# A step's sum over head groups and its turn as one fp32 product with a selector, in a recurrent attention kernel

## The chip, the cores and the metric

One core of a Trainium2 chip runs the whole program. The metric is the device time of one execution in microseconds (us); the time of a kernel is the median of several executions. Engines are named as in the profile: PE is TensorE's matrix multiplication and PEld its weight load, DVE is VectorE, ACT is ScalarE, POOL is GpSimd, SP is the engine that issues most DMAs.

## The reference, cut to what matters

The reference is one forward and backward pass of a layer that adds three things: the input, a squared-ReLU feed-forward block on the normalised input, and an attention that runs over 64 segments of 32 rows, each with 8 rows of memory that the segment before it has made. The gradients of all inputs are returned as well, so the recurrence is run once forward and once backward.

```python
for s in range(n_seg):                       # 64 segments, one after the other
    xs = x[:, s * seg_len:(s + 1) * seg_len, :].copy()
    h = jnp.concatenate([mem, xs], axis=1)   # 8 + 32 rows of 512
    q = jnp.einsum('btd,dhe->bhte', h, Wq)   # 32 heads of 128
    k = jnp.einsum('btd,dhe->bhte', h, Wk)
    v = jnp.einsum('btd,dhe->bhte', h, Wv)
    scores = jnp.einsum('bhqe,bhke->bhqk', q, k) * scale
    scores = jnp.where(mask[None, None], scores, -1000000000.0)
    p = _softmax(scores, axis=-1)
    o = jnp.einsum('bhqk,bhke->bhqe', p, v)
    o = jnp.einsum('bhte,hed->btd', o, Wo)   # a sum over the 32 heads
    mem = o[:, :M, :].copy()                 # the next segment starts from this
    outs.append(o[:, M:, :])
```

The last product is a sum over all 32 heads. Its first 8 rows are what the next segment waits for. In the backward pass the gradient of the memory goes the other way, segment 63 first, and the sum over heads (of the products with Wq, Wk and Wv turned) closes each step in the same way.

## The kernel before, in words

The program has five stages: the feed-forward block; its weight gradients; the forward recurrence; a short pass over left-over rows; the backward recurrence; and last the attention's weight gradients. On the timeline of the profile the forward recurrence lies at about 423 to 1342 us and the backward one at about 1578 to 2545 us.

A recurrence has 64 steps, in 16 blocks of 4 (`SPB` is 4, `NB` 16). In a step the 32 heads lie as 4 groups of 8 (`HG` is 4): partitions 32g to 32g + 31 hold the 32 rows of group g. A step projects its rows (`proj`, line 421, 4 column tiles at a time), turns them (`flip`, line 165), makes scores (`scores`, line 442), softmax or its gradient on DVE and ACT (`soft_ops`, `ds_ops`), the products with the values (`outer`, line 549) and the product with the output weights (`gather`, line 462). `gather` leaves in the PSUM tile `ps_R` (forward) or `ps_gR` (backward) 128 rows of 512: for each group g its own partial sum over 8 heads, 32 rows each.

The end of a step makes of this the turned sum over the groups. Its operations, by their names in the order lists:

- `ra`, `rb`: the two halves of the 128 x 512 partial sums are copied from PSUM to the fp32 tile `R4` ("R" in the profile), one by DVE (line 408), one by ACT (line 405), one after the other. Which half comes first differs from step to step.
- `ta`, `tb` (`turn_ops`, line 471): four fp32 transposes by TensorE, two for each half, into one PSUM tile `ps_sum` of 128 x 512. Column c * 128 + 32g + r of it belongs to chunk c of the model dimension, group g, row r.
- `HT` (`over_groups`, line 484): one DVE sum over g of rows 0 to 7 into the next step's input (`X` forward, `GT` backward). The next step's projections wait for it.
- `xt` (`over_groups` again): the same for rows 8 to 31 into the block's fp32 tile `XT` (`b_XT` backward).

The 8 memory rows of four steps are also handled once per block together ("left" rows, order names with `L.`): `L.ta` and `L.tb` make the same four transposes from `R4L` or `b_R`, and `L.xt` (`left_sums`, line 478) sums them with four DVE instructions.

The order of all this is written out by hand: `F_ORDER` and `B_ORDER` list the names of the operations for the four steps of a block, `play` calls them in that order, and each engine gets its instructions in it. A `+` or `-` behind a name moves it to another step; `L.` names belong to the block. What is put behind `ta` and `tb` in these lists (a gather of left rows of 8 or 16 matmuls, `L.G0` or `L.H1` and the like, a score `L.S1+`, products `L.W1+`) runs on TensorE while DVE does `HT`. `on_engines` says which copies are done by ACT and which by DVE. PSUM tiles named by `big` and `tr` share four banks that are given out in turn.

```python
"L.ta kl k1fl soN-- k0Te q1Te L.tb s0 ..."          # forward, fourth step, left products among the flips
"... qg1 rb L.G3 L.ldt+ tb ra ta L.H3 HT"           # backward, third step's end
"ldk- ldp- vp0 L.ko0 vp1 s0 L.tb- L.ldk L.xt- d10"  # backward, a block's first step: L.xt stands before d10 on DVE
```

`d10` to `d40` are the four DVE instructions of the scores' gradient (lines 498 to 508).

Of the kernel before, what the change touches and what calls it, by code (L numbers as in the profile page):

```python
# [8 lines left out]
ALU = mybir.AluOpType  # L9
AX = mybir.AxisListType  # L10
BF16 = mybir.dt.bfloat16
F32 = mybir.dt.float32
P = 128
# [13 lines left out]
def kernel(  # L27
# [27 lines left out]
    nc = tc.nc  # L55

    _, S, D = A_x.shape
    M = A_mem0.shape[1]
    H, Dh = A_Wq.shape[1], A_Wq.shape[2]
    F = B_w1.shape[1]  # L60
    SEG = int(A_seg_len)
    assert Dh == P and D % P == 0 and F % P == 0 and S % P == 0 and D <= 512
    L = M + SEG
    assert L <= 64 and P % SEG == 0
    NSEG = S // SEG
    DC = D // P
    TC = S // P
    HD = H * Dh
    SPB = P // SEG
# [29 lines left out]
    const = ctx.enter_context(tc.tile_pool(name="const", bufs=1))  # L99
# [3 lines left out]
    HG = 4  # L103
# [48 lines left out]
    nc.vector.memset(ones_col[:], 1.0)  # L152
    identF = const.tile([P, P], F32, name="identF")
    nc.vector.tensor_copy(identF[:], ident[:])
    rstd_t = const.tile([P, TC], F32, name="rstd_t")

    def sb(name, bufs, side=None):
# [12 lines left out]
    HT = htp.tile([P, DC, S], BF16, name="HT")  # L170
# [8 lines left out]
    with sb("p1", 1) as p1, sb("p1b", 2) as p1b:  # L179
# [64 lines left out]
        for rb in range(NRB):  # L244
# [4 lines left out]
            for fc in range(FC):  # L249
                ps = pst([P, RB], F32, name="ps_h1")  # L250
                for dc in range(DC):
                    nc.tensor.matmul(ps[:], lhsT=W1[:, dc, fc * P:(fc + 1) * P], rhs=HT[:, dc, r0:r0 + RB],
                                     start=(dc == 0), stop=(dc == DC - 1))
                nc.scalar.activation(rT[:, fc, :], ps[:], ACT.Relu, bias=b1T[:, fc:fc + 1], scale=1.0)
                nc.vector.tensor_tensor(out=aT[:, fc, :], in0=rT[:, fc, :], in1=rT[:, fc, :], op=ALU.mult)
            for fc in range(FC):
                ps2 = pst([P, RB], F32, name="ps_ga")
                for dc in range(DC):
                    nc.tensor.matmul(ps2[:], lhsT=W2T[:, dc, fc * P:(fc + 1) * P], rhs=gT[:, dc, r0:r0 + RB],
                                     start=(dc == 0), stop=(dc == DC - 1))  # L260
# [23 lines left out]
            for rc in range(RCB):  # L284
                rr0 = r0 + rc * P
                psB = pst([P, D], F32, name="ps_B")
                for fc in range(FC):
                    nc.tensor.matmul(psB[:], lhsT=aT[:, fc, rc * P:(rc + 1) * P], rhs=W2[:, fc, :],
                                     start=(fc == 0), stop=(fc == FC - 1))
# [6 lines left out]
                for fc in range(FC):  # L296
                    nc.tensor.matmul(psG[:], lhsT=gh1T[:, fc, rc * P:(rc + 1) * P], rhs=W1T[:, fc, :],
                                     start=(fc == 0), stop=(fc == FC - 1))
# [3 lines left out]
                for srcT, dstD in ((aT, S_AN), (gh1T, S_GH1N)):  # L302
                    Nt = p1b.tile([P, F], BF16, name="Nt", tag="Nt")
                    for (f0b, nb) in GRPF8:
                        ps = pst([P, nb * P], BF16, name="ps_trf")
# [13 lines left out]
    with sb("p2", 1) as p2:  # L319
# [5 lines left out]
        with sb("p2r", 1, "right") as p2r:  # L325
# [19 lines left out]
            ps = pst([1, D], F32, name="ps_gb2")  # L345
# [120 lines left out]
    def turn_ops(o, alloc, R4, st):  # L466

        def tT(c):
            if "T" not in st:
                st["T"] = alloc("ps_sum")  # L470
            nc.tensor.transpose(st["T"][:, c * P:(c + 1) * P], R4()[:, c * P:(c + 1) * P], identF[:])  # L471
        for h in range(2):
            o["t%s" % "ab"[h]] = lambda h=h: [tT(c) for c in (2 * h, 2 * h + 1)]

    def left_sums(XT, T):

        for c in range(DC):
            nc.vector.tensor_reduce(XT[:, c, :, 0:M], T[:, c * P:(c + 1) * P].rearrange("p (g j t) -> p j t g", g=HG, j=SPB),
                                    axis=AX.X, op=ALU.add)

    def over_groups(out, T, rows):

        with nc.allow_low_precision(reason="summed in float32, rounded once on the way out"):
            nc.vector.tensor_reduce(out, T[:].rearrange("p (c g r) -> p c r g", c=DC, g=HG)[:, :, rows], axis=AX.X,  # L484
                                    op=ALU.add)

    def block_rows(ps, XT):

# [94 lines left out]
    def play(order, n, steps, lefts, step, blk, last={}):  # L583
# [34 lines left out]
        "ob1+ L.tu1+ g1+ ra+ soP+ ws+ L.u0 soN L.W0+ L.BT rb+ L.E0+ L.E1+ ta+ tb+ L.ob0+ soN+ L.W1+")  # L618
    ENGS = on_engines(
        "L.E0 L.E1 L.E3 L.E4 L.E5 L.oa1 L.ob1 k0ev k1ev oa0 ob0 ob1 q0ev q1Te q1ev rb v0ev v1ev",  # L620
        "L.E2 L.oa0 L.ob0 L.pm0 L.pm1 L.ra k0Te k1Te oa1 pm0 pm1 q0Te ra we")
    with sb("fw", 1) as fw, psum("fr", 4) as fr, psum("fpp", 1) as fpp, \
            ExitStack() as fstack:

# [45 lines left out]
        def block(b):  # L670

            if b not in blk:
                shapes = {"kL": (fs, [P, KH, HG, NL], BF16), "OT": (fs, [P, HG, KH, SPB, SEG], BF16),
                          "X": (fs, [P, DC, P], BF16),
                          "kM": (fo, [P, KH, HG, NL], BF16), "vTM": (fo, [P, KH, HG, NL], BF16),
                          "XT": (fs, [P, DC, SPB, SEG], F32), "qL": (fo, [P, KH, HG, NL], BF16),
                          "VL": (fo, [P, GW], BF16), "vM": (fo, [P, GW], BF16), "EL": (fo, [P, KH, KW], BF16),
                          "OTL": (fo, [P, KH, HG, NL], BF16),
                          "bb": (fo, [P, D], BF16)}

                def make(n):
                    pool, shape, dt = shapes[n]
                    return pool.tile(shape, dt, name=n, tag=n)
                blk[b] = Tiles(make)
            return blk[b]
# [114 lines left out]
        def fwd(s):  # L800
# [88 lines left out]
            def HTf():  # L889
                if s + 1 < NSEG:  # L890
                    b1, j1 = divmod(s + 1, SPB)
                    over_groups(block(b1)["X"][:, :, j1 * SEG:j1 * SEG + M], st["T"], slice(0, M))
            o["HT"] = HTf
            o["xt"] = lambda: over_groups(B_["XT"][:, :, j, M:SEG], st["T"], slice(M, SEG))
            t, h0 = divmod(2 * s, H)

            def wt():
# [58 lines left out]
    with sb("ls", 3) as ls, sb("lo", 1) as lo_, psum("lpp", 1) as lpp, psum("lr", 4) as lr:  # L956
# [99 lines left out]
        "o1mm+ o0fl+ L.qo0+ L.ta o0te+ o1ev+ L.ko1+")  # L1056
    ENGS = on_engines(
        "L.ra0 kea0 kea1 keb0 kla0 klb0 o0ev o1ev o1te qea0 qea1 rb vea veb vla vlb",
        "keb1 kla1 klb1 o0te qeb0 qeb1 ra")
    with sb("bq", 1) as bq, sb("bs", 2) as bs, sb("bt", 1) as bt, psum("bpp", 1) as bpp, psum("br", 4) as br:  # L1060
        G4 = {n: bq.tile([P, HG, KH, SPB, SEG], BF16, name="g" + n) for n in "vkq"}
        gS = bq.tile([P, KH, KW], BF16, name="gS")
# [96 lines left out]
        def bwd(s):  # L1159
# [106 lines left out]
            def HTf():  # L1266
                if s > 0:
                    b1, j1 = divmod(s - 1, SPB)
                    over_groups(gts[b1][:, :, j1 * SEG:j1 * SEG + M], st["T"], slice(0, M))
                else:  # L1270
                    ps["S0"] = bq.tile([P, DC, M], F32, name="gm0")
                    over_groups(ps["S0"][:], st["T"], slice(0, M))
            o["HT"] = HTf

            def xtf():
                over_groups(B_["XT"][:, :, j, M:SEG], st["T"], slice(M, SEG))
            o["xt"] = xtf
            o["S0"] = lambda: ps["S0"]
            return o
# [170 lines left out]
```

## Time and profile before

| What | Value |
|---|---|
| median of 7 runs | 3193.85 us (3180.56 to 3206.58) |
| the profiled execution | 3186.18 us, span 3184.4 us |
| mean granted TensorE clock | 0.943 of full speed |
| PE busy, matmuls | 2726.6 us (86%), 51480 |
| PEld busy, weight loads | 1393.5 us (44%), 51480 |
| DVE busy, instructions | 1250.4 us (39%), 3503 |
| ACT busy, instructions | 1019.3 us (32%), 2370 |
| DMA engines | 594.37 MB, 187 GB/s in the mean |

The table is of one profiled execution. A busy share is a share of the span; TensorE's matmuls are pipelined, so that its busy time says that it had work, not that it ran at its peak. In a line of the groups, such as "L471 PE MATMUL ps_sum<-identF,R 128*128 128x128 f32 x512 | 100.3, 295 | 22.6 <-ACT R L405 16.1", stand the line of the program, the engine, the operation, what it writes and reads, its shape, the number of instructions, their busy time in us, the mean length of one in ns, and the engine's idle time just before them with what ended most of it. In the view of a tile the three numbers are the shortest, median and longest length in ns. On the timeline the first number is the start in us, the second the length from the first to the last end of the instructions that the line stands for.

### The profile page before, as it was taken

The numbers are of one execution on the slowest core, as the hardware profiler recorded it, in microseconds if no ns is written. First come the engines' busy times: TensorE is split into PE (matmuls) and PEld (weight loads), VectorE is DVE, ScalarE is ACT, GpSimd is POOL, SyncE is SP. The second block draws the span as 40 slices with busy tenths as digits, with TensorE's granted clock in tenths as the row PEclk, the third lists the DMA queues.
The fourth block names the chain that finished last, engine by engine and source line by source line (L and its number), as shares of the span: only waits on it lengthen the run. The fifth ranks groups of instructions, "written<-read, shape, count | busy, mean of one in ns | idle before, by whom it ended". The sixth has DMA issues, their size and how long they took to land.

```text
span 3184.4 us, 115139 instructions
## 1 busy us (share of the span) xinstructions
PE 2726.6 (86%) x51480; PEld 1393.5 (44%) x51480; DVE 1250.4 (39%) x3503; ACT 1019.3 (32%) x2370; POOL 329.7 (10%) x601
## 2 busy tenths in 40 slices
PE   8998789999999988635688888898899847999998
PEld 4553345545555544312344444444444423444443
DVE  5540055556666656423344444444445400010011
ACT  2331144444445444212333333333333201111111
POOL 0000010000000000000122222222122100000000
PEclk9999899999999999766799999999999978999999
DMA  9358636667677766689666777677677599999993
GB/s 255 124 131 311 241 110 183 194 179 196 175 195 195 194 181 155 205 209 251 164 156 185 174 168 187 173 166 185 169 174 184 160 251 196 215 190 220 188 185 90
DMA packets 827697, 594.37 MB, mean 187 GB/s; under 512 B 595633, under 2 KB 705346, under 8 KB 824002
## 3 DMA queue, kind: packets, MB, share of 16 engines
q1 hardware_dynamic: 809794, 532.47, 67.5%
q0 software_dynamic: 17408, 54.54, 5.8%
q8 instruction: 403, 6.60, 0.9%
q14 instruction: 92, 0.75, 0.1%
HBM read 205.14 MB, written 250.10 MB: 143 GB/s over the span
## 4 chain that ended last, share of the span: by engine, by line
PE 63%; DMA 11%; SPq 8%; DVE 8%; ACT 5%; issue 4%; POOL 0%; ACTq 0%; POOLq 0%; DVEq 0%
PE ps_gw L1411 13%; PE ps_proj L421 12%; PE ps_gR L462 9%; PE b_pp L549 4%; PE ps_sum L471 3%; SPq L1336 3%; DMA S_GOL<-l_gON 3%; PE ps_R L462 3%; PE ps_L L382 2%; PE ps_tr L165 2%; PE ps_RL L1115 2%; PE ps_w L341 2%; PE ps_w L361 2%; PE ps_sc L442 1%; PE f_pp L549 1%
## 5 line engine op out<-in xcount | busy, mean ns | idle before, releaser
L1411 PE MATMUL ps_gw<-gn,HNc 128*128 128x512 bf16 x1920 | 416.7, 379 | 3.4 <-ACT wt L1386 3.4
L421 PE MATMUL ps_proj<-Wqkv,X 128*32 128x512 bf16 x6144 | 367.2, 389 | 16.6 <-DVE X L484 6.9
L1411 PEld LDWEIGHTS <-HNc 128*128 128x128 bf16 x1920 | 187.8, 98 | 227.6 <-issue 4.0
L405 ACT CAST f_N<-ps_proj 128x512 bf16<-128x512 f32 x384 | 218.6, 587 | 188.6 <-PE ps_proj L421 178.8
L1386 ACT CAST wt<-ps_gw 128x512 bf16<-128x512 f32 x126 | 69.6, 591 | 547.4 <-DMA out_dram<-wt 310.1
L421 PEld LDWEIGHTS <-X 128*32 128x32 bf16 x6144 | 161.2, 98 | 172.5 <-issue 20.3
L1369 DVE TENSOR_TENSOR gx<-ps_rows,gb 128x512 f32<-128x512 f32 x16 | 11.1, 692 | 434.4 <-PE ps_rows L1367 434.4
L1411 PE MATMUL ps_gw<-GOc,gn 128*128 128x512 bf16 x640 | 141.9, 385 | 28.1 <-DMA gn<-S_ON 28.1
L462 PE MATMUL ps_gR<-WT,gv 128*32 128x512 bf16 x2048 | 149.2, 386 | 9.2 <-ACT gOT L405 4.2
L462 PE MATMUL ps_gR<-WT,gk 128*32 128x512 bf16 x2048 | 142.4, 397 | 11.4 <-ACT gk L405 6.0
L462 PE MATMUL ps_gR<-WT,gq 128*32 128x512 bf16 x2048 | 143.7, 402 | 5.6 <-issue 5.4
L421 PE MATMUL ps_proj<-WoT,GT 128*32 128x512 bf16 x2048 | 124.0, 384 | 5.1 <-POOL GT L1145 4.0
L405 ACT CAST gON<-ps_proj 128x512 bf16<-128x512 f32 x128 | 75.0, 586 | 166.2 <-PE ps_proj L421 166.2
L462 PE MATMUL ps_R<-Wo,OT 128*32 128x512 bf16 x2048 | 123.1, 382 | 0.0
L471 PE MATMUL ps_sum<-identF,R 128*128 128x128 f32 x512 | 100.3, 295 | 22.6 <-ACT R L405 16.1
L829 POOL COPY kM<-f_kT 128x256 bf16<-128x256 bf16 x64 | 25.8, 403 | 831.0 <-DVE f_kT L408 831.0
L382 PE MATMUL ps_L<-Wqkv,XL 128*128 128x512 bf16 x384 | 96.9, 388 | 16.6 <-DMA XL<-S_XL 16.6
L1411 PEld LDWEIGHTS <-gn 128*128 128x128 bf16 x640 | 63.4, 99 | 105.5 <-DMA gn<-S_ON 28.4
L405 ACT CAST gk<-b_pp 128x256 bf16<-128x256 f32 x192 | 65.9, 381 | 134.3 <-PE b_pp L549 126.2
L471 PEld LDWEIGHTS ps_sum<-identF,R 128*128 128x128 f32 x512 | 55.3, 142 | 84.8 <-ACT R L405 59.3
L408 DVE COPY R<-ps_gR 128x256 f32<-128x256 f32 x64 | 27.2, 425 | 162.3 <-ACT R L405 118.4
L405 ACT CAST OT<-f_pp 128x256 bf16<-128x256 f32 x192 | 65.2, 374 | 63.4 <-PE f_pp L549 62.4
(221 smaller groups left out, 4659.8 us busy)
## 6 DMA issues: line engine op xcount, KB each, us to landing
S_A<-f_N SPq DMA_DIRECT2D x64, 512.0 KB
out_dram<-wt SPq DMA_DIRECT2D x154, 128.0 KB
S_A<-f_N SPq DMA_DIRECT2D x64, 256.0 KB
S_ON<-OC SPq DMA_DIRECT2D x64, 256.0 KB
b_qN<-S_A POOLq DMA_DIRECT2D x64, 256.0 KB, 4.3
b_kN<-S_A POOLq DMA_DIRECT2D x64, 256.0 KB, 4.0
S_GB<-gv SPq DMA_DIRECT2D x32, 512.0 KB
S_GB<-gq SPq DMA_DIRECT2D x32, 512.0 KB
```

Source lines behind the costliest of these rows:

```text
L165: nc.tensor.transpose(ps_ap, in_ap, ident[base:base + k, base:base + k])
L341: nc.tensor.matmul(ps[:], lhsT=aN[:, rc, fc * P:(fc + 1) * P], rhs=gN[:, rc, :], start=(rc == 0), stop=(rc == TC - 1))
L361: nc.tensor.matmul(ps[:, 0:nf], lhsT=xnN[:, rc, dc * P:(dc + 1) * P], rhs=gh1N[:, rc, f0:f0 + nf], start=(rc == 0), stop=(rc == TC - 1))
L382: nc.tensor.matmul(ps[:], lhsT=x(dc), rhs=Wqkv[:, dc, c0:c0 + 512], start=(dc == 0), stop=(dc == DC - 1))
L405: nc.scalar.copy(out, in_)
L421: nc.tensor.matmul(ps[32 * g:32 * g + 32, :], lhsT=hT[:, dc, :], rhs=W[:, dc, c:c + 4 * P], start=(dc == 0), stop=(dc == DC - 1), tile_pos ...
L462: nc.tensor.matmul(R[32 * g:32 * g + 32, :], lhsT=XT(k, g), rhs=W[:, g * KH + k, :], start=(first and k == 4 * h), stop=(last and k == 4 * ...
L471: nc.tensor.transpose(st["T"][:, c * P:(c + 1) * P], R4()[:, c * P:(c + 1) * P], identF[:])
L549: nc.tensor.matmul(o, lhsT=N_[32 * g:32 * g + m, kk * P:(kk + 1) * P], rhs=X(kk)[32 * g:32 * g + m], start=(i == 0), stop=(i == len(jobs) ...
L1336: nc.sync.dma_start_transpose(t_[:, b, :].rearrange("p (k e) -> p k e", k=KH), blocks(b)[:, g].rearrange("p k r -> p (k r)"))
L1386: nc.any.tensor_copy(wt[:], ps[:])
L1411: nc.tensor.matmul(ps[:], lhsT=l(rc), rhs=r(rc), start=(n == 0), stop=(n == RC_ALL - 1))
```

## The change

`sel` is a 128 x 32 fp32 tile: four 32 x 32 identities under each other, made at the start by one DVE sum over the four column groups of the identity. In place of a transpose, each chunk of `R4` becomes the stationary operand of a true fp32 matmul with `sel` as the moving one: this turns the chunk and sums the four groups at once, and leaves 32 columns in place of 128. `HT`, `xt` and `L.xt` then only copy from PSUM; they stay on DVE (`HT xt L.xt` are added to the DVE names of both stages), and `L.xt` is one copy in place of four sums. The order lists are not changed. Line numbers of the changed program are higher by 2 above this place and lower by 2 below it.

```diff
--- before.py
+++ after.py
@@ -152,6 +152,8 @@
     nc.vector.memset(ones_col[:], 1.0)
     identF = const.tile([P, P], F32, name="identF")
     nc.vector.tensor_copy(identF[:], ident[:])
+    sel = const.tile([P, SEG], F32, name="sel")
+    nc.vector.tensor_reduce(sel[:], identF[:].rearrange("p (g r) -> p r g", g=HG), axis=AX.X, op=ALU.add)
     rstd_t = const.tile([P, TC], F32, name="rstd_t")
 
     def sb(name, bufs, side=None):
@@ -468,21 +470,17 @@
         def tT(c):
             if "T" not in st:
                 st["T"] = alloc("ps_sum")
-            nc.tensor.transpose(st["T"][:, c * P:(c + 1) * P], R4()[:, c * P:(c + 1) * P], identF[:])
+            nc.tensor.matmul(st["T"][:, c * SEG:(c + 1) * SEG], lhsT=R4()[:, c * P:(c + 1) * P], rhs=sel[:],
+                             start=True, stop=True, skip_group_check=True)
         for h in range(2):
             o["t%s" % "ab"[h]] = lambda h=h: [tT(c) for c in (2 * h, 2 * h + 1)]
 
+    def rows_of_sum(T, rows):
+        return T[:, 0:DC * SEG].rearrange("p (c r) -> p c r", c=DC)[:, :, rows]
+
     def left_sums(XT, T):
 
-        for c in range(DC):
-            nc.vector.tensor_reduce(XT[:, c, :, 0:M], T[:, c * P:(c + 1) * P].rearrange("p (g j t) -> p j t g", g=HG, j=SPB),
-                                    axis=AX.X, op=ALU.add)
-
-    def over_groups(out, T, rows):
-
-        with nc.allow_low_precision(reason="summed in float32, rounded once on the way out"):
-            nc.vector.tensor_reduce(out, T[:].rearrange("p (c g r) -> p c r g", c=DC, g=HG)[:, :, rows], axis=AX.X,
-                                    op=ALU.add)
+        ENGS["L.xt"](XT[:, :, :, 0:M], T[:, 0:DC * SEG].rearrange("p (c j t) -> p c j t", c=DC, j=SPB))
 
     def block_rows(ps, XT):
 
@@ -618,7 +616,7 @@
         "ob1+ L.tu1+ g1+ ra+ soP+ ws+ L.u0 soN L.W0+ L.BT rb+ L.E0+ L.E1+ ta+ tb+ L.ob0+ soN+ L.W1+")
     ENGS = on_engines(
         "L.E0 L.E1 L.E3 L.E4 L.E5 L.oa1 L.ob1 k0ev k1ev oa0 ob0 ob1 q0ev q1Te q1ev rb v0ev v1ev",
-        "L.E2 L.oa0 L.ob0 L.pm0 L.pm1 L.ra k0Te k1Te oa1 pm0 pm1 q0Te ra we")
+        "L.E2 L.oa0 L.ob0 L.pm0 L.pm1 L.ra k0Te k1Te oa1 pm0 pm1 q0Te ra we HT xt L.xt")
     with sb("fw", 1) as fw, psum("fr", 4) as fr, psum("fpp", 1) as fpp, \
             ExitStack() as fstack:
 
@@ -889,9 +887,9 @@
             def HTf():
                 if s + 1 < NSEG:
                     b1, j1 = divmod(s + 1, SPB)
-                    over_groups(block(b1)["X"][:, :, j1 * SEG:j1 * SEG + M], st["T"], slice(0, M))
+                    ENGS["HT"](block(b1)["X"][:, :, j1 * SEG:j1 * SEG + M], rows_of_sum(st["T"], slice(0, M)))
             o["HT"] = HTf
-            o["xt"] = lambda: over_groups(B_["XT"][:, :, j, M:SEG], st["T"], slice(M, SEG))
+            o["xt"] = lambda: ENGS["xt"](B_["XT"][:, :, j, M:SEG], rows_of_sum(st["T"], slice(M, SEG)))
             t, h0 = divmod(2 * s, H)
 
             def wt():
@@ -1056,7 +1054,7 @@
         "o1mm+ o0fl+ L.qo0+ L.ta o0te+ o1ev+ L.ko1+")
     ENGS = on_engines(
         "L.ra0 kea0 kea1 keb0 kla0 klb0 o0ev o1ev o1te qea0 qea1 rb vea veb vla vlb",
-        "keb1 kla1 klb1 o0te qeb0 qeb1 ra")
+        "keb1 kla1 klb1 o0te qeb0 qeb1 ra HT xt L.xt")
     with sb("bq", 1) as bq, sb("bs", 2) as bs, sb("bt", 1) as bt, psum("bpp", 1) as bpp, psum("br", 4) as br:
         G4 = {n: bq.tile([P, HG, KH, SPB, SEG], BF16, name="g" + n) for n in "vkq"}
         gS = bq.tile([P, KH, KW], BF16, name="gS")
@@ -1266,14 +1264,14 @@
             def HTf():
                 if s > 0:
                     b1, j1 = divmod(s - 1, SPB)
-                    over_groups(gts[b1][:, :, j1 * SEG:j1 * SEG + M], st["T"], slice(0, M))
+                    ENGS["HT"](gts[b1][:, :, j1 * SEG:j1 * SEG + M], rows_of_sum(st["T"], slice(0, M)))
                 else:
                     ps["S0"] = bq.tile([P, DC, M], F32, name="gm0")
-                    over_groups(ps["S0"][:], st["T"], slice(0, M))
+                    ENGS["HT"](ps["S0"][:], rows_of_sum(st["T"], slice(0, M)))
             o["HT"] = HTf
 
             def xtf():
-                over_groups(B_["XT"][:, :, j, M:SEG], st["T"], slice(M, SEG))
+                ENGS["xt"](B_["XT"][:, :, j, M:SEG], rows_of_sum(st["T"], slice(M, SEG)))
             o["xt"] = xtf
             o["S0"] = lambda: ps["S0"]
             return o
```

## The prediction

> **What bounds the kernel now.** I read the page first (shares, chain, groups), then the view of the tile ps_sum, then the timeline around single step ends, and last the waits.
>
> The page's chain of work that ended last, and two groups of line 471:
>
> ```profile
> PE 63%; DMA 11%; SPq 8%; DVE 8%; ACT 5%; issue 4%; POOL 0%; ACTq 0%; POOLq 0%; DVEq 0%
> L471 PE MATMUL ps_sum<-identF,R 128*128 128x128 f32 x512 | 100.3, 295 | 22.6 <-ACT R L405 16.1
> L471 PEld LDWEIGHTS ps_sum<-identF,R 128*128 128x128 f32 x512 | 55.3, 142 | 84.8 <-ACT R L405 59.3
> ```
>
> TensorE carries most of the chain. Each step of the two recurrences ends with four fp32 transposes, and their weight loads wait for the copies of R: this is the serial end of a step, where TensorE has little else to do. The view of ps_sum, and one row of the view of b_gkL (min/median/max in ns), give the prices:
>
> ```profile
> L471 PEld LDWEIGHTS ps_sum<-identF,R x512: 137/140/230, 423.1 to 2536.9; 128*128 128x128 f32 x171
> L471 PE MATMUL ps_sum<-identF,R x512: 269/273/421, 423.1 to 2537.0; 128*128 128x128 f32 x171
> L478 DVE TENSOR_REDUCE b_XT<-ps_sum x64: 278/281/293, 1688.0 to 2545.0; 128x32 f32<-128x128 f32 x64
> L484 DVE TENSOR_REDUCE b_XT<-ps_sum x64: 545/548/549, 1578.4 to 2537.5; 128x96 f32<-128x384 f32 x64
> L484 DVE TENSOR_REDUCE GT<-ps_sum x63: 290/292/294, 1578.0 to 2521.9; 128x32 bf16<-128x128 f32 x63
> ...
> L408 DVE CAST b_gkL<-b_pp x128: 211/215/226, 1573.8 to 2534.0; 128x64 bf16<-128x64 f32 x128
> ```
>
> A step end of the backward recurrence on the timeline:
>
> ```profile
> 1649.94 0.37 ACT L405 COPY R<-ps_gR 128x256 f32<-128x256 f32 x1 [2.04 <-PE ps_gR L462]
> 1650.35 0.42 DVE L408 COPY R<-ps_gR 128x256 f32<-128x256 f32 x1 [2.16 <-ACT R L405]
> 1650.37 0.20 PEld L471 LDWEIGHTS ps_sum<-identF,R 128*128 128x128 f32 x2 [0.59 <-ACT R L405]
> 1650.37 0.90 PE L471 MATMUL ps_sum<-identF,R 128*128 128x128 f32 x4
> 1650.83 0.20 PEld L471 LDWEIGHTS ps_sum<-identF,R 128*128 128x128 f32 x2 [0.26 <-DVE R L408]
> ...
> 1651.20 0.61 PE L1115 MATMUL ps_RL<-WT,b_gkL 128*32 128x512 bf16 x8
> 1651.30 0.29 DVE L484 TENSOR_REDUCE GT<-ps_sum 128x32 bf16<-128x128 f32 x1 [0.53 <-PE ps_sum L471]
> 1651.51 0.55 DVE L484 TENSOR_REDUCE b_XT<-ps_sum 128x96 f32<-128x384 f32 x1
> ...
> 1651.65 0.34 PEld L421 LDWEIGHTS <-GT 128*32 128x32 bf16 x12 [0.33 <-DVE GT L484]
> ```
>
> See three things. Two loads of 140 ns take 0.20 us together, so the second starts 57 ns after the first. The sum into GT (HT in the order) starts 37 ns after the last transpose and the next projection's load 54 ns after its end. Between lies a gather of eight matmuls that fills TensorE almost exactly until then.
>
> **Part 1, TensorE.** No engine's order of work changes; in the built program each of the 640 transposes (one load, one matmul of 128 columns) becomes two loads and two matmuls of 32 columns, the high and the low half of the fp32 weights. What do eight such pairs take? A matmul's length here is a fixed part and a part per column: bf16 matmuls of 512 and 40 columns take 379 and 181 ns, 0.42 ns a column and 164 ns fixed. The fp32 transpose's 273 ns is then 109 ns of streaming, 0.85 a column: two passes. Single starts on the timeline are 109 ns apart, so the transposes go at the pace of their matmuls. A load of 32 columns takes 97 ns and the fp32 load of 128 takes 140: 43 ns for 96 columns, about 57 for 128, which is also the distance of two load starts. A 32-column product with two passes streams for some 27 ns, so the pairs should go at the pace of their loads, 57 ns. No fp32 product is in this trace, so I bound the pace: 57 ns below (two load starts), 109 above (two transposes). I take 57, the row of the same load.
>
> Then eight pairs take 8 x 57 = 456 ns against 57 + 4 x 109 = 493, and the last one ends after 164 + 27 = 191 instead of 273. Where both halves of R are there (copy on VectorE first), the last result comes 9 ns earlier; in the form shown, where the last two products wait for VectorE's copy, 440 ns become 4 x 57 + 191 = 419: 21 earlier. TensorE itself is free 6 and 16 ns earlier.
>
> The Trainium skill, "TensorE: Matmul & The Clock Gate", section "LDWEIGHTS (loading the stationary operand)", gives columns / 1.2 GHz, an estimate of 107 ns for 128 columns; the two load starts 57 ns apart speak against it at full clock, and by that rule the sum would be that of the first rival. "Perfetto Trace Analysis", section "Transposes", says that a logical transpose should not be a standard matmul; no row here prices that choice, and it speaks against the change.
>
> **Part 2, VectorE.** Copies from PSUM cost a fixed part and about 1.09 ns an element: 215 ns for 64 elements, 424 for the 256 of R. So HT's 32 elements take about 180 instead of 292 (-112), xt's 96 about 250 instead of 548, and the left sums 128 elements about 285 instead of four sums that take 884 together. The new sum that builds sel is one instruction of some 0.3 us at the start.
>
> **Part 3, what lies on the path.** I went through the 126 step ends on the timeline.
> - Open ends, 41: the projection waits for HT alone (second and fourth steps of a forward block, six first ones, four others). Gain 9 or 21 plus 112, about 0.12 each: 4.9 us.
> - Covered ends: in 60 backward ones the eight-matmul gather lets go at about 336 ns after HT's start and HT at 346. HT's gain is cut off at 10 ns, TensorE's 16 (45 ends) or 6 (15 ends) come to it: 45 x 0.026 + 15 x 0.016 = 1.4 us. In 15 forward ends a gather of 16 runs until 766 ns: 15 x 0.016 = 0.2.
> - Ten forward ends wait for ScalarE's copy dN, which waits for a DMA: 0.
> - The shorter xt is followed by idle VectorE or by work that waits for something else: 0. If that cover were gone, 0.3 us a step.
> - Left products: two products at a time, 4 x 57 + 27 = 255 against 57 + 218 = 275: nothing.
> - Left sums backward, 15 blocks, here in the timeline:
>
> ```profile
> 1688.01 0.88 DVE L478 TENSOR_REDUCE b_XT<-ps_sum 128x32 f32<-128x128 f32 x4 [0.96 <-PE ps_sum L471]
> ...
> 1688.81 0.31 DVE L498 TENSOR_TENSOR ds_t<-ps_sc,b_P 128x160 f32<-128x160 f32 x1
> ...
> 1689.13 1.05 PE L462 MATMUL ps_gR<-WT,gv 128*32 128x512 bf16 x16 [0.39 <-ACT gOT L405]
> ...
> 1689.87 0.32 DVE L508 SCALAR_TENSOR_TENSOR gS<-ds_t,b_P 128x160 bf16<-128x160 f32 x1
> 1689.99 0.28 PE L442 MATMUL ps_sc<-b_vT,gOT 128*32 128x40 bf16 x16
> ```
>
> The scores' gradient waits behind the four sums. Its four instructions start 0.6 us earlier, but TensorE has the gather of gv, which waits for ScalarE, and the second scores before it needs gS: about 0.2 us come through (next products at 1690.34, scores done by 1690.13). 15 x 0.2 = 3.1 us.
>
> Sum: 4.9 + 1.4 + 0.2 + 3.1 = 9.6 us earlier. The profiled execution took 3186.18 us (span 3184.4 and 1.8 around it), 7.7 below the median of 3193.85; so it would take 3176.6, and the median 3184. That is 0.3%; about 0.5% (16 us) is what a measurement of this kernel can tell from no change.
>
> **Rivals.** *Slower: loads at 109 ns.* If the loads of the halves do not overlap the short matmuls, or load more slowly than the transposes' loads, TensorE at the step end becomes the bound. Price at 109: 23 open ends +0.03 (second half only), 11 open ends where TensorE is busy until late +0.23, 7 with both halves at hand +0.25; covered ends 45 x 0.127 + 15 x 0.35 backward, 10 x 0.34 + 5 x 0.14 forward; 47 pairs of left products in dense TensorE work x 0.14; less 3.1 of the left sums: 0.7 + 2.5 + 1.7 + 10.9 + 4.1 + 6.5 - 3.1 = 23 us later, 3217. It decides from a pace of about 72 ns on (9.6 of the 33 us between 57 and 109). For it: no row shows this product. Against it: the load's 140 ns and the 57 ns.
>
> *Faster by more: the freed VectorE counts.* All of the 0.6 us in 15 backward blocks (9.3 instead of 3.1), and as much in the 16 forward blocks, where the left sums stand before the copy of OT (9): 3184 - 6 - 9 = 3169. Against it: in the forward blocks ScalarE's half of that copy starts only 45 ns before VectorE's, so TensorE is the limit.
>
> *No gain at all: the longer program.* In the waits, TensorE stands without a releaser:
>
> ```profile
> PEld L549 <- issue: 188.4, 244, 13.8
> ```
>
> All such rows of PE and PEld come to some 390 us; 1,280 more instructions on 102,960 are 1.2%, so 5 us more if these stalls go with the number of instructions. Their places move with every added instruction, so I allow 8 us both ways. With it the gain falls below what can be measured, 3189.
>
> **How the numbers follow.** Likeliest case 0.50 (3184, its own range 3174 to 3194), the longer program 0.10, more gain 0.15 (3169), slower loads 0.25 (3217). The range reaches into both outer cases, with the run-to-run spread and the 8 us of moved stalls: 3164 to 3224. Faster by over 0.5% (below 3178): most of the third case and a quarter of the first, 0.27. Slower (above 3210): the last one, and stalls, 0.25. Same 0.48.
>
> **What would show it.** In the changed profile: 1,280 loads and matmuls on the products' line where 640 were; loads about 140 ns, starts 57 apart (109 would be the first rival); the matmuls about 190 ns; HT as a copy of about 180; xt about 250. In the step shown, the projection's first load some 25 ns earlier after VectorE's copy of R, and 120 at the open ends. The gradient of the scores 0.6 us earlier after the left products. I am wrong if the products' matmuls are much longer than 200 ns, or if the stalls move by more than 8 us.

## The result and the profile after

The changed kernel takes 3213.16 us (median of 13 runs) where the kernel before takes 3189.47 (median of 32): the ratio is 1.0075, with a 95% interval from 1.0057 to 1.0093. It is slower by about 24 us. The prediction said 3184 and "same" as the likeliest; the time lies in its range, but on the side of the rival "loads at 109 ns" (3217). The profiled execution took 3217.39 us (span 3215.5, mean granted clock 0.939).

The chain of work that ended last, and the two groups of the products, on the page of the changed kernel:

```profile
PE 63%; DMA 11%; SPq 10%; DVE 7%; ACT 5%; issue 4%; POOL 0%; ACTq 0%; POOLq 0%; DVEq 0%
L473 PEld LDWEIGHTS ps_sum<-sel,R 128*128 128x128 f32 x1024 | 131.2, 196 | 63.4 <-ACT R L407 58.4
L473 PE MATMUL ps_sum<-sel,R 128*128 128x32 f32 x1024 | 139.6, 281 | 21.1 <-ACT R L407 16.1
```

TensorE's share of the chain has not changed. The loads for the turn have gone from 55.3 to 131.2 us of busy time: twice as many, and each of them longer. The view of the tile ps_sum (shortest, median and longest length in ns) gives the prices that the prediction had to guess:

```profile
L473 PEld LDWEIGHTS ps_sum<-sel,R x1024: 186/192/338, 423.4 to 2561.8; 128*128 128x128 f32 x171
L473 PE MATMUL ps_sum<-sel,R x1024: 192/276/403, 423.4 to 2561.8; 128*128 128x32 f32 x171
...
L410 DVE COPY b_XT<-ps_sum x80: 246/248/292, 1600.8 to 2570.1; 128x96 f32<-128x96 f32 x64, 128x128 f32<-128x128 f32 x16
...
L410 DVE CAST GT<-ps_sum x63: 191/192/194, 1600.5 to 2546.8; 128x32 bf16<-128x32 f32 x63
```

VectorE's side came as forecast: HT 192 ns, xt 248, the left copy 292. TensorE's did not: a load of one half takes 192 ns where a transpose's load took 140, and a product's matmul 276 where 191 was expected. The timeline shows what this makes of the step end that the prediction showed (the backward end at 1649.94 us):

```profile
1732.98 0.42 DVE L410 COPY R<-ps_gR 128x256 f32<-128x256 f32 x1 [2.16 <-ACT R L407]
1733.00 0.98 PEld L473 LDWEIGHTS ps_sum<-sel,R 128*128 128x128 f32 x8 [0.59 <-ACT R L407]
1733.00 1.09 PE L473 MATMUL ps_sum<-sel,R 128*128 128x32 f32 x8
1734.03 0.62 PE L1113 MATMUL ps_RL<-WT,b_gkL 128*32 128x512 bf16 x8
1734.13 0.19 DVE L410 CAST GT<-ps_sum 128x32 bf16<-128x32 f32 x1 [0.72 <-PE ps_sum L473]
...
1734.38 1.06 PEld L423 LDWEIGHTS <-GT 128*32 128x32 bf16 x24 [0.23 <-DVE GT L410]
```

Eight loads take 0.98 us, first start to last end. That is 7 x 112 ns between starts and 192 for the last load; 960 of the 1,280 load starts lie 108 to 112 ns behind the one before. HT, which waits for the last result, starts 0.73 us after VectorE's copy of R has ended (1733.40 to 1734.13), not 0.53 as before. HT gives 0.10 back, and GT is ready 0.92 us after that copy instead of 0.82.

Where the time is, the stages say. The view by windows gives for the forward recurrence of before (first line) and after (second), from the first HT to the last: length, busy time and count of PE, PEld, DVE, ACT and POOL, granted clock, DMA share, GB/s.

```profile
423.90:1307.10 883.20, 820.53 (x18542) 443.42 (x18546) 523.81 (x1545) 417.67 (x921) 49.94 (x124) 0.98 0.66 180
424.50:1330.40 905.90, 853.14 (x18847) 486.35 (x18850) 491.85 (x1503) 417.38 (x921) 49.93 (x124) 0.97 0.64 175
```

The forward recurrence is 22.7 us longer in these two executions and the backward one 2.3 (959.3 and 961.6). Part of the forward difference is the granted clock. This is why the comparisons below are also given without it. The mean granted clock of each execution is known, and time x (1 - clock) is at most what the clock has cost it. Among 29 executions of the kernel before, the times scatter with a standard deviation of 7.6 us, and what is left without that loss with 5.6. The column "rest" below is an estimate made in this way, from means, good to some 4 to 6 us. Since it takes off the most that the clock can have cost, the worth of a change lies, but for this scatter, between the column of the difference and that of the rest.

### The profile page after: what moved, and what is told of

Read it like the earlier page. It is cut to its first block, busy times and chain, and to the rows that moved or that the text cites. A ratio compares the mean times of both kernels' runs of the same rounds, so it can differ in the third digit from the quotient of the medians.

```text
span 3215.5 us, 116324 instructions
## 1 busy us (share of the span) xinstructions
PE 2779.6 (86%) x52120; PEld 1488.3 (46%) x52120; DVE 1183.1 (37%) x3408; ACT 1018.7 (32%) x2370; POOL 329.7 (10%) x601
## 4 chain that ended last, share of the span: by engine, by line
PE 63%; DMA 11%; SPq 10%; DVE 7%; ACT 5%; issue 4%; POOL 0%; ACTq 0%; POOLq 0%; DVEq 0%
PE ps_gw L1409 12%; PE ps_proj L423 11%; PE ps_gR L464 9%; PE ps_sum L473 5%; SPq L1334 4%; PE b_pp L547 4%; DMA S_GOL<-l_gON 3%; PE ps_R L464 3%; PE ps_tr L167 2%; PE ps_L L384 2%; PE ps_RL L1113 2%; PE ps_w L343 2%; DMA vM<-S_A 2%; PE ps_w L363 2%; DMA out_dram<-wt 1%
## 5 line engine op out<-in xcount | busy, mean ns | idle before, releaser
L423 PE MATMUL ps_proj<-Wqkv,X 128*32 128x512 bf16 x6144 | 374.2, 394 | 10.3 <-DVE X L410 5.1
L473 PEld LDWEIGHTS ps_sum<-sel,R 128*128 128x128 f32 x1024 | 131.2, 196 | 63.4 <-ACT R L407 58.4
L473 PE MATMUL ps_sum<-sel,R 128*128 128x32 f32 x1024 | 139.6, 281 | 21.1 <-ACT R L407 16.1
L464 PEld LDWEIGHTS <-gq 128*32 128x32 bf16 x2048 | 56.4, 100 | 62.9 <-issue 18.8
```

Of the source, the lines that this page charges most:

```text
L423: nc.tensor.matmul(ps[32 * g:32 * g + 32, :], lhsT=hT[:, dc, :], rhs=W[:, dc, c:c + 4 * P], start=(dc == 0), stop=(dc == DC - 1), tile_pos ...
L464: nc.tensor.matmul(R[32 * g:32 * g + 32, :], lhsT=XT(k, g), rhs=W[:, g * KH + k, :], start=(first and k == 4 * h), stop=(last and k == 4 * ...
L473: nc.tensor.matmul(st["T"][:, c * SEG:(c + 1) * SEG], lhsT=R4()[:, c * P:(c + 1) * P], rhs=sel[:], start=True, stop=True, skip_group_check ...
```

## The experiments

**The theories.** A: the loads of the halves set the pace at the end of a step, 112 ns each, and the copies on VectorE give back about what the prediction said. B: something else costs the time (the matmuls, the longer program). Two parts were tested apart, first the whole vector part and the whole product part, then each by its place.

| kernel | time, us (kernel before, measured beside it) | ratio, 95% interval | difference of means, us | of it granted clock | rest |
|---|---|---|---|---|---|
| the change | 3213.2 (3189.5) | 1.0075 [1.0057, 1.0093] | +24 | +3 | about +20 |
| e2 copies only | 3165.1 (3189.7) | 0.9918 [0.9894, 0.9941] | -28 | -9 | -19 |
| e3 products only | 3248.2 (3189.7) | 1.0169 [1.0140, 1.0197] | +53 | +19 | +34 |
| e6 HT copy | 3186.4 (3190.5) | 0.9994 [0.9974, 1.0013] | -3 | +2 | -5 |
| e7 xt copy | 3173.6 (3190.5) | 0.9957 [0.9937, 0.9978] | -16 | -8 | -8 |
| e8 left copy | 3183.9 (3190.5) | 0.9977 [0.9954, 1.0000] | -9 | +1 | -10 |
| e9 left products | 3203.0 (3204.5) | 1.0003 [0.9982, 1.0024] | 0 | +3 | -3 |
| e10 step products | 3234.6 (3204.5) | 1.0109 [1.0070, 1.0148] | +33 | +12 | +21 |
| e5 float32r | 3160.8 (3190.5) | 0.9921 [0.9896, 0.9945] | -29 | 0 | -30 |
| e11 bf16 turn | 3183.7 (3204.5) | 0.9936 [0.9913, 0.9958] | -20 | +1 | -22 |
| e4 bf16 product | 3141.4 (3189.7) | 0.9839 [0.9814, 0.9865] | -53 | -3 | -50 |

e9, e10 and e11 ran on another chip, where the kernel before itself takes 3204.5 us, so only ratios and differences can be compared between rows. For the first row the clock of the kernel before is taken from the runs beside the other rows.

**e1_wide_sel: is it the loads or the matmuls?** The selector twice as wide, so that each matmul has 64 columns in place of 32:

```diff
-    sel = const.tile([P, SEG], F32, name="sel")
+    sel = const.tile([P, 2 * SEG], F32, name="sel")
...
-            nc.tensor.matmul(st["T"][:, c * SEG:(c + 1) * SEG], ..., rhs=sel[:], ...)
+            nc.tensor.matmul(st["T"][:, c * P:c * P + 2 * SEG], ..., rhs=sel[:], ...)
```

> The selector is 64 columns wide, two copies of the 32-column one side by side, and the second copy's result is not read; all else is the changed kernel. Theory (loads): in the changed kernel a weight load of one half of a true fp32 operand lasts 192 ns where the transposes' load lasted 140, and the pairs go at the pace of these loads, 112 ns. Then a matmul twice as wide (64 columns instead of 32) hides behind the next load as before: start to start stays 112 ns, a step's last result comes some 27 ns later, and the time stays within 5 us of the changed kernel's 3213. Rival (matmuls): the 276 ns that the profile gives to the 32-column matmul are its own, 112 ns of streaming for 32 columns; then 64 columns take 224 ns, start to start doubles, and eight of them add 0.9 us to each of 126 step ends, over 80 us in all.

One execution: 3216.45 us, as the change. 976 of 1,280 load starts are 108 to 112 ns apart (960 in the change); the load takes 192 ns, the matmul 275. Doubling the columns changed no pace, so the matmuls' columns do not set it. That the loads do is seen where TensorE has waited before a turn. There the second load starts 108 or 109 ns after the first in both kernels, though the second matmul starts 160 ns after the first in e1 and some 132 in the change; the transposes' second load starts 56 to 64 ns after the first.

**e2_copies_only and e3_products_only: the two parts apart.** e2 keeps the transposes and puts copies of group 0 in place of the sums; e3 has the products, and VectorE sums as long as before (each result read four times):

```diff
# e2, on the kernel before
-            nc.vector.tensor_reduce(out, T[:].rearrange("p (c g r) -> p c r g", ...)[:, :, rows], axis=AX.X, op=ALU.add)
+            nc.vector.tensor_copy(out, T[:].rearrange("p (c g r) -> p c g r", ...)[:, :, 0, rows])
# e3, on the changed kernel
-                    ENGS["HT"](block(b1)["X"][...], rows_of_sum(st["T"], slice(0, M)))
+                    over_groups(block(b1)["X"][...], rows_of_sum(st["T"], slice(0, M)))   # reduce of src.unsqueeze(3).to_broadcast(.., HG)
```

> The kernel before with its fp32 transposes, where HT, xt and the left sums only copy the rows of head group 0 (the sum over groups 1 to 3 is left out): VectorE's part of the change alone. The prediction's vector term: 41 open step ends by 0.112 us, 60 covered ends by 0.010, 15 backward blocks by 0.2: 4.6 + 0.6 + 3.1 = 8.3 us faster than before, ratio 0.9974. Rival (the freed VectorE counts for more): all of the 0.6 us at the left sums in 31 blocks, 20 us faster or more, ratio 0.993. Rival (no gain from VectorE): within 3 us.

> The changed kernel with its fp32 products, where HT, xt and the left sums are sums as long as before (each adds the same 32 columns four times, so the values are four times too large): TensorE's part of the change alone. Theory (loads at 112 ns): what the change lost, about 24 us, and what VectorE's part gained, some 8, are both seen here: 32 us slower than before, ratio 1.010. Rival (the longer program's instruction stalls): about 5 us slower. If the two parts do not add up, this one and the copies alone will not sum to the change's +24.

The parts have opposite signs and together give the change: -28 + 53 = +25. Both came out larger than expected. Without the granted clock, the products cost 34 us. The prediction's rival comes to some 31 for them at 109 ns (its 23 and the 8 that the copies were to give). The copies are worth 19 where the prediction had 8. So theory A holds for the products and fails on the copies.

**e6_ht_copy, e7_xt_copy, e8_left_copy: which copy gives the time?** Each on the kernel before, each replacing one of the three sums by the copy of e2:

```diff
# e6 (rows.start == 0: HT) and e7 (rows.start > 0: xt), in over_groups
+        if rows.start == 0:
+            nc.vector.tensor_copy(out, T[:].rearrange("p (c g r) -> p c g r", c=DC, g=HG)[:, :, 0, rows])
+            return
# e8, in left_sums, in place of the four sums
+        nc.vector.tensor_copy(XT[:, :, :, 0:M], T[:].rearrange("p (c g j t) -> p c g j t", ...)[:, :, 0])
```

> The kernel before, with its fp32 transposes, but HT copies the 8 memory rows of group 0 (a copy, some 190 ns for 292) instead of summing the four groups; xt and the left sums sum as before. Left out: groups 1 to 3 in the memory rows. The run with all three copies was 26 us faster than before where the prediction's VectorE terms give 8. Accounting of the prediction: 41 open ends x 0.11 us + 60 covered ends x 0.01 = 5 us faster, ratio 0.998. Rival 'HT is on the path at every end': 126 x 0.10 = 13 us faster or more, ratio 0.996. If this is 0.998 the rest of the 26 us lies in xt and the left sums.

> The kernel before, but xt copies rows 8 to 31 of group 0 (some 250 ns for 548) instead of summing; HT and the left sums as before. Left out: groups 1 to 3 in the output rows. Accounting of the prediction: 0, ratio 1.000 (what stands behind xt on VectorE waits for something else). Rival 'the cover is gone in part': the prediction named 0.3 us a step if the cover is gone; in 48 of the 126 steps that is 14 us faster, ratio 0.9955.

> The kernel before, but one copy of group 0 (some 290 ns) in place of the four left sums (884 ns); HT and xt as before. Left out: groups 1 to 3 in the left rows. Accounting of the prediction: 15 x 0.2 = 3 us faster, ratio 0.999. Rival 'the freed VectorE counts' of the prediction: 0.6 us in 31 blocks, 18 us faster, ratio 0.994. If neither this nor the copies of HT and xt alone is faster by much, the three gains need each other.

HT agrees with its forecast of 5 us (rest -5), though its interval includes no gain at all. xt, forecast at nothing, gives 16 us (8 without the clock); the left copy 9 to 10 where 3.1 was forecast, with an interval that ends at no gain. The traces show one place for each, which accounts for a part. First xt, at the end of a block's first forward step: four lines of the timeline of before (first step of the twelfth block), then three of e7.

```profile
1051.18 1.07 ACT L405 CAST dN<-ps_L 128x512 bf16<-128x512 f32 x2 [1.80 <-DMA S_WT<-wtt]
1051.18 0.29 DVE L484 TENSOR_REDUCE X<-ps_sum 128x32 bf16<-128x128 f32 x1 [0.18 <-PE ps_sum L471]
1051.39 0.55 DVE L484 TENSOR_REDUCE XT<-ps_sum 128x96 f32<-128x384 f32 x1
...
1051.82 1.05 PE L421 MATMUL ps_proj<-Wqkv,X 128*32 128x512 bf16 x16 [0.37 <-ACT dN L405]
```

```profile
931.97 0.29 DVE L487 TENSOR_REDUCE X<-ps_sum 128x32 bf16<-128x128 f32 x1 [0.18 <-PE ps_sum L471]
932.18 0.25 DVE L484 COPY XT<-ps_sum 128x96 f32<-128x96 f32 x1
932.48 2.99 PE L421 MATMUL ps_proj<-Wqkv,X 128*32 128x512 bf16 x52 [0.25 <-DVE XT L484]
```

The projection needs only X, but in e7 it starts when xt ends, though it reads nothing that xt writes: its PSUM tile has the bank (the piece of PSUM that one tile fills) that ps_sum leaves, and xt is the last to read ps_sum. In ten blocks (first steps 8 to 44) it starts 0.51 us after HT's start in e7, 0.71 in e6, 0.81 in e3, and 0.41 in e2 and in the changed kernel: 0.05 after the end of xt in each, whatever HT and xt take. In the kernel before it does not wait for xt: in the first fence it starts 0.12 us before xt's end, released by ScalarE's copy dN (two copies in 1.07 us). With dN the ten ends vary from 0.35 to 1.37 us, 0.74 in the mean. The built programs say why. At these ends the next step's first projection tile waits for ScalarE in before, e8 and e9, at ten of ten; in e2, e3, e6, e7, e10 and the change it is the second tile that does. The two have changed banks, although the order of work is the same. For e7 this makes 10 x 0.23 = 2.3 us (0.74 less 0.51); the rest of its gain was not traced to a place.

Then the left copy, at a block's first backward step. The lines of the changed kernel answer to those at 1688.01 us in the prediction:

```profile
1709.12 0.29 DVE L410 COPY b_XT<-ps_sum 128x128 f32<-128x128 f32 x1 [1.35 <-PE ps_sum L473]
...
1709.33 0.31 DVE L496 TENSOR_TENSOR ds_t<-ps_sc,b_P 128x160 f32<-128x160 f32 x1
...
1710.39 0.33 DVE L506 SCALAR_TENSOR_TENSOR gS<-ds_t,b_P 128x160 bf16<-128x160 f32 x1
...
1710.86 0.20 PE L547 MATMUL b_pp<-gS,b_qN 32*128 32x40 bf16 x4
```

The products with gS, the finished gradient of the scores, start 1.74 us after the copy's start; in the kernel before they start 2.33 us after the first of the four sums, in each of the 14 blocks found in its trace. In 12 of 14 blocks of the change and of e8 it is 1.74. There all of the 0.59 us comes through, which would be 8.9 us in 15 blocks. In the two other blocks of e8 they start 3.1 and 3.3 us after it, behind waits without a releaser, and its whole backward recurrence is only 2.2 us shorter than before in the profiled executions (957.1 and 959.3). So it is not shown that e8's 9 us come from these blocks. The prediction had let only 0.2 through, since the gather of gv and the scores behind it hold TensorE until then. That was so with the banks of before, where the gather waits for ScalarE's copy gOT and starts 0.05 us after its end, mostly 1.12 us after the first sum. In most blocks of e8 it starts 0.63 us after the copy's start, before gOT has ended (1.07). The built programs show the same here as for xt: in before, e3, e6, e7 and e10 the gather's tile waits for ScalarE at this place in 14 of 14 blocks, in e8, e9 and the change for VectorE. With a left sum of another length the gather has got the bank that this sum leaves.

**e9_left_product and e10_step_product: where is the loss?** The change in the left rows alone and in the steps alone (turn_ops gets a flag that chooses product or transpose):

```diff
-    def turn_ops(o, alloc, R4, st):
+    def turn_ops(o, alloc, R4, st, left=False):
...
+            if left:        # e10: if not left
+                nc.tensor.matmul(st["T"][:, c * SEG:(c + 1) * SEG], lhsT=R4()[:, c * P:(c + 1) * P], rhs=sel[:], ...)
+                return
             nc.tensor.transpose(...)
```

> The change in the left rows alone: L.ta and L.tb are products with the selector and L.xt one copy; the steps keep transposes and sums. Accounting with the measured pace (load starts 112 ns apart): 31 blocks with two pairs of chunks, each pair four loads x 112 = 448 ns where two transposes took 275, so up to 0.17 x 62 = 11 us later where TensorE is full, less the 7 us that the left copies alone gave: 0 to 4 us later, ratio 1.000 to 1.001. Rival 'the left products carry the loss, as they stand in dense TensorE work': 15 us later or more, ratio 1.005.

> The change in the steps alone: ta and tb are products, HT and xt copies; the left rows keep transposes and four sums. If the loss lies in the step ends: 94 ns at an open end and more at a covered one, the change's 24 us less what the left rows take, so 20 to 27 us later, ratio 1.006 to 1.008. Rival (loss in the left rows): 5 to 10 us later, ratio 1.002 to 1.003.

The left rows are even: what the products cost there, the single copy returns. The loss is that of the step ends (+33, or +21 without the clock). That the two kinds of load differ is seen in e9, where both stand in one execution:

```profile
L477 PEld LDWEIGHTS ps_sum<-identF,R x512: 137/140/231, 425.1 to 2542.3; 128*128 128x128 f32 x171
L474 PEld LDWEIGHTS ps_sum<-sel,b_R x128: 186/192/338, 1692.8 to 2550.3; 128*128 128x128 f32 x128
```

One clean kind of end shows the price where TensorE is dense. At the end of a block's third forward step four transposes 109 ns apart became eight pairs 112 ns apart, and from the second step's HT to the third's it takes 0.35 us longer in e3. In the changed kernel it is 0.25, since HT's copy at the second step gives 0.10 back.

**e5_fp32r: four bytes, but one load a chunk.** R4 and the selector are declared float32r, 4 bytes as before:

```diff
-    sel = const.tile([P, SEG], F32, name="sel")
+    sel = const.tile([P, SEG], F32R, name="sel")
...
-                    st["R4"] = fo.tile([P, D], F32, name="R4", tag="R4s")
+                    st["R4"] = fo.tile([P, D], F32R, name="R4", tag="R4s")
```

> The changed kernel, but R4 and the selector hold their four bytes as float32r, which asks for one pass over the weights instead of a high and a low half. Theory 'two loads of 192 ns, 112 ns apart, for each chunk set the pace': if a chunk is one load and one matmul, four pairs replace eight, the last product of a step is about 0.2 us earlier at an end in the form 'VectorE's copy last', and the time falls below before, to about 3155 (ratio 0.988, near the bf16 run's 0.984). Rival 'the pace is a price of the four-byte type, not of the second pass': loads of twice the length, ratio 1.00 to 1.01, as the change.

The view of ps_sum of this kernel:

```profile
L475 PEld LDWEIGHTS ps_sum<-sel,R x512: 186/189/192, 424.8 to 2507.7; 128*128 128x128 f32 x171
L475 PE MATMUL ps_sum<-sel,R x512: 262/263/367, 424.8 to 2507.8; 128*128 128x32 f32 x171
```

Half as many loads, each as long as in the changed kernel, and 29 us faster than before. The load of 190 ns is thus the price of 128 columns of this four-byte kind, and the change pays it twice for each chunk. Undoing only the second pass, a load and a matmul for each chunk, turns +24 into -29.

**e4_bf16 and e11_bf16_turn: is it the type or the product?** e4 is the changed kernel with R4 and the selector in bfloat16, e11 the kernel before with R4 in bfloat16, so with transposes and sums. Both round the partial sums to bf16 before they are summed:

```diff
-                    st["R4"] = fo.tile([P, D], F32, name="R4", tag="R4s")
+                    st["R4"] = fo.tile([P, D], BF16, name="R4", tag="R4s")
...
-            nc.tensor.transpose(st["T"][...], R4()[...], identF[:])     # e11
+            transpose_to(st["T"][...], R4()[...])
```

> The changed kernel with R4 and the selector in bf16 (the partial sums are rounded to bf16 before the sum over the groups): each product is one load and one matmul. Theory (loads): a bf16 load of 128 columns and a matmul of 32 go at 30 to 60 ns a pair; the four products of a step take about 0.2 us in place of 0.9, the last result in the form with VectorE's copy last comes some 0.18 us earlier than in the kernel before, and HT 0.1 earlier: about 0.28 at 41 open ends, 0.13 to 0.35 at 75 covered ends, 3 at the left sums: 25 to 30 us faster than before, ratio 0.992, and 50 faster than the changed kernel. If the cost were not in TensorE's pairs but in the stalls or in VectorE's copies, the time would stay near the changed kernel's.

> The kernel before with R4 in bfloat16: bf16 transposes into a bf16 PSUM tile, and HT, xt and the left sums still sum over the groups on VectorE (292, 548 and 884 ns). Rounds the partial sums to bf16 before the sum. The bf16 product was 51 us faster than before, the copies alone 26. Theory 'the four-byte type costs the step end its time, the product is only a way to it': bf16 loads (97 ns for 140, starts under 30 ns apart) and transposes of 128 columns at 0.42 ns a column (218 ns for 273) give 0.15 us an end, some 19 to 25 us faster, ratio 0.992 to 0.994. Rival 'it needs the 32 columns of the product': 0 to 6 us faster, ratio 0.998 to 1.000.

The matmuls in the views of ps_sum of e4 and of e11:

```profile
L474 PE MATMUL ps_sum<-sel,R x512: 176/176/234, 421.0 to 2487.0; 128*128 128x32 bf16 x171
```

```profile
L165 PE MATMUL ps_sum<-ident,R x512: 217/219/246, 424.2 to 2531.4; 128*128 128x128 bf16 x171
```

e4 beats both kernels, by 1.6% against before, and gains twice the 25 to 30 us that were expected. e11 gains 20 us with the sums still on VectorE, as the theory of the type said; e4 gains 33 us more, of which the copies would explain most (28 in e2) and the shorter product the rest, but no run takes these two apart in bf16. At an end with VectorE's copy of R last, the time from that copy's end to HT's end goes with the result: 0.92 us with the change, 0.82 before, 0.68 with float32r, 0.67 in e11 and 0.50 in e4. It is not the whole of it: in e7 it is 0.82 as before, and e7 is 16 us faster.

## Why the prediction was wrong, by its own steps

**Part 1, the pace: this step failed.** The counts were right: 1,280 loads and matmuls for 640. The pace of 57 ns came from two load starts of the transposes, "the row of the same load". It is not the same load: in e9's trace the transposes' take 140 ns and those of the halves 192. The load starts are 108 to 112 ns apart, next to the other bound (109). The prediction's second support for 57, that 96 columns more make a load 43 ns longer, was a misreading: the 97 ns were of a bf16 load, and in the kernel before a bf16 load takes as long for 128 columns as for 32. Two groups of its backward recurrence (count, busy us, mean ns, idle time before):

```profile
L421 PEld LDWEIGHTS <-GT 128*32 128x32 bf16 x2016 | 48.0, 96 | 63.1 <-DVE GT L484 21.9
L165 PEld LDWEIGHTS <-gON 128*128 128x128 bf16 x504 | 29.6, 98 | 21.8 <-ACT gON L405 13.2 <-issue 6.4
```

So the 43 ns went with the type or the kind of load, not with the columns. The decision was therefore made by the choice between two bounds that had been named, 57 and 109, with 72 as the point from which it turns. The result of the last matmul was expected 191 ns after its start and takes 276. After VectorE's copy of R the last result was to come 21 ns earlier; it comes 0.19 us later (HT starts at 0.73 for 0.53). In the sum, products that were to gain just over 1 us (9.6 less the 8.3 of the copies) cost 34 to 53.

The Trainium skill, "TensorE: Matmul & The Clock Gate", section "LDWEIGHTS (loading the stationary operand)", gives columns / 1.2 GHz, 107 ns for 128 columns. The loads of the halves, 112 ns from start to start, agree with it; the transposes' loads, 57 ns apart, do not. Its section "Weight-path perf modes — Fast Weight Load (FWL) and DoubleRow" says that the fast weight load is not used for FP32; e4 and e5 agree in so far as two loads that follow each other freely start 15 ns apart in bf16 and 108 or 109 in float32r; the fp32 transposes' 57 ns lie between and are not explained by it. "Perfetto Trace Analysis", section "Transposes", says that a transpose should not be done as a standard matmul. e3 gives the price in this kernel: 53 us (34 without the clock) for 640 of them in fp32. In bf16 it does not decide here: e4, with a product that also saves the sums, is faster than e11, with the transpose.

**Part 2, the copies: right.** 192, 248 and 292 ns were forecast as 180, 250 and 285.

**Part 3, the path: one term right, two too small.** The open ends: 4.9 us forecast, of which some 4.6 were HT's; e6 shows 5 without the clock, not clear of the noise. "The shorter xt: 0" failed: at ten first forward steps the projection's bank comes from xt after the change. The ten forward ends put down to ScalarE's dN at no gain were read rightly for the kernel before, but the change took that wait away. The left sums, 3.1 us: in 12 of 14 blocks all of the 0.59 us came through, not 0.2, because the gather of gv got another bank and no longer stood in between. "No engine's order of work changes" was true, and still the waits changed: four banks are shared, and which tile gets which of them is not a fixed turn, as the description of the kernel has it, but differs between these programs, in which only the instructions that fill and free such a bank are others.

**The rivals.** "Loads at 109 ns" was the right mechanism and nearly the right size, 23 us later against 24. The agreement is in part chance: its some 31 us for the products are near e3's rest (34), but its gain on VectorE, 8 us, was less than half of the 19 in e2's rest, the granted clock adds some 3 us in the change, and its +0.03 us at 23 open ends is 0.09 where VectorE's copy of R comes last (0.92 for 0.82). "The freed VectorE counts" was right as well in the backward blocks, place by place (0.59 us for 0.6); its 9 us in the forward blocks do not show in the profiled executions (883.8 us in e8, 883.2 before). The two rivals had been put as alternatives and came together. The longer program went the other way: the waits without a releaser at the value products (line 549 before, 547 after) fell from 188.4 to 177.7 us, and all such rows of TensorE, the prediction's some 390, from 392 to 368. That is 24 us less, more than the 8 us either way that the prediction allowed. Waits that became fewer do not explain a slower kernel, and e5, at 363, has about as many as the change, so they do not separate these two either.

**What stays open.** The products on their own came with a lower granted clock (e3 0.936, e10 0.938 in the mean of their executions, 0.941 before), the copies with a higher one (e2 0.943, e7 0.944, before 0.941 to 0.942). Why, no run here tells; a chance difference of the executions is not excluded. Of xt's 8 to 16 us only some 2 were traced to a place. Nor is it told why the change loses so little in the backward recurrence: its profiled execution takes 961.6 us there (959.3 before), where e10, with the same step ends, takes 985.9. The waits of TensorE without a releaser in this stage are 182 us in the change, 215 before and 225 in e10; what part of that is on the path was not tried. No run changed the banks alone, so what they are worth by themselves was not tried.

## What to carry to other kernels

Before an fp32 transpose is turned into an fp32 product, count loads and not columns: here each chunk went from one load to two of 192 ns, 112 ns apart, and that cost more at the serial end of a step than all that VectorE was relieved of. A price may be taken from another instruction only if it is the same one in kind and mode; where the bounds of one unknown price lie on both sides of the decision, the likeliest case is no safer than the other. And when a reader of a PSUM tile gets shorter, compare the waits of the two built programs and not only the order: who waits for the bank can change with it, as it did here at ten forward and 14 backward places.

## What the runs showed of the hardware that was not expected

- A load of 128 columns of four bytes takes 140 ns for a transpose, 192 for a half of an fp32 product and 189 for float32r. The starts lie some 57, 112 and 109 ns apart where loads follow each other freely. A bf16 load takes 96 to 98 ns, for 32 columns as for 128.
- An fp32 product's matmul of 32 columns takes 276 ns and one of 64 columns 275; the float32r one of 32 columns takes 263, the bf16 one 176.
- Two executions that do the same TensorE work differ in granted clock by up to 0.02 over the forward recurrence (0.98 in e8, 1.00 in e7, which take 883.8 and 868.0 us there), as much as the effects under study, so that a time is to be read with its clock beside it.
